# A third tile routine for an expert's last tokens: x stationary in column groups of TensorE, and the counts that choose it

## The chip, the core and the metric

The kernel runs on one core of a Trainium2 chip. The metric is the device time of one execution in microseconds (us); before the change the median of 4 runs is 718.03 us (716.1 to 719.92). All operands of the matrix products discussed here are float32.

## What is computed

Sliding-window causal attention (8 batches, 8 heads, 576 positions, head width 64, window 64) gives x with 4608 tokens of 512 numbers. Each token then goes to one of 8 experts, and its row passes through that expert's two weight matrices:

```python
logits = x @ w_gate                      # 4608 x 8
expert_idx = argmax(logits, axis=1)
gate_w = softmax(logits)[chosen]
for e in range(8):                       # x_e: the tokens of expert e
    h = maximum(x_e @ w1[e], 0.0)        # 512 -> 1024
    y_e = h @ w2[e]                      # 1024 -> 512
out = gate_w[:, None] * y                # in the tokens' own order
```

The inputs are drawn from a fixed seed. Counted from the reference with them, experts 0 to 7 get 669, 400, 748, 505, 592, 390, 566 and 738 tokens. In tiles of 256, expert by expert, the last tile holds 157, 144, 236, 249, 80, 134, 54 and 226 of them.

## The kernel before, in words

The first part, up to some 226 us, does the attention with PE (TensorE), ACT, DVE and POOL side by side, and writes x, weighted by the gate, to device memory (`x_dram`). It also counts the tokens of each expert (`count`), and `starts` (L216 to L225) turns the counts into numbers of tiles on DVE with small 128x8 instructions: per expert the number of whole tiles (`fulls_i`), of all tiles (`all_i`), the largest of these, and the place where each expert's tiles begin. Two tiles of expert 0 are worked in straight code, mixed with the end of the routing, among it the table of which token lies in which slot (`slot_table`: L839 to L864, read by PE at L854).

From some 272 us on, the rest of the tiles is chosen at run time. `expert(e)` (L1063) issues the loads of expert e+1's weights on SP's queue, does its first tile (none for expert 0, which has two already), and `more` (L1074) tests registers that hold the counts: is there another tile, and is it a whole one or a half one? Each test is a branch on every engine. Four places matter:

- **A whole tile** of 256 slots (`hidden`, `output`): seven products of half-size blocks for each of the two matrix products, with the sums of weight blocks formed beforehand by POOL (`sums_w1`, `sums_w2`: four instructions each) and the sums of x by DVE (`sums_x`, L333). The weights stand in TensorE (128 columns each) and x moves for the first product; the hidden values stand and the weights move for the second (L388).
- **A half tile** for up to 160 left-over tokens (`half_tile`, L436 to L477): plain products. For the first, w1 stands and 160 tokens move (L444). For the second, the 32 tokens behind the first 128 stand in one of four 32-column groups at a time while 128 columns of w2 move through each (L465); then the 128 tokens stand and all 512 columns of w2 move (L470). Both accumulate over the 8 blocks of the hidden width.
- **The feed for the next tile.** Inside tile n, DVE turns the rows of tile n+1 in 16 32x32-block transposes (`turned_blocks`, L315), ACT copies them into place (`keep_turned`, L327), DVE forms their sums (`sums_x`), and POOL then gathers the rows of tile n+2 into the buffer just turned (`gather`, L275). One buffer of rows exists, so the gather waits for the last transpose.
- **The results of the last tile.** At a tile's start `finish` (L425) adds the last product of the tile before on DVE (three L384 instructions); POOL scatters the rows to the output (`scatter`, L295) after it. Then, if it is the expert's second tile, POOL forms the sums of the next expert's w1, or, if it is an expert's first, those of its own w2.

The order on each engine is the order of the code; there is no scheduler. A float32 matmul has two records on PE in this trace and two on PEld (the loads of weights).

Of the kernel before, what the change touches and what calls it, by code (L numbers as in the profile page):

```python
# [13 lines left out]
I32 = mybir.dt.int32  # L14
AF = mybir.ActivationFunctionType
ALU = mybir.AluOpType
AX = mybir.AxisListType
# [19 lines left out]
def kernel(  # L37
# [34 lines left out]
    NW = 2  # L72
    QD = 32
    HALF = P + QD
    NCUT = NT // P
    assert D == WINDOW and 2 * D == P and NG * P == DM and NB * WINDOW == S
    assert S - SM == WINDOW and KB == NV + 1 and NTB * P == BG * S and B % BG == 0 and NTILE * TB <= 128 * P
# [10 lines left out]
    wg = consts.tile([P, NG, GE], F32, name="wg")  # L88
    nc.gpsimd.memset(wg[:], 0.0)
    perm_i = consts.tile([P, NS], I32, name="perm_i")  # L90
    info_i = consts.tile([P, 2 * E + 1], I32, name="info_i")
    fulls_i, all_i, most_i = info_i[:, 0:E], info_i[:, E : 2 * E], info_i[:, 2 * E :]

    places_i = consts.tile([P, E + 1], I32, name="places_i")
    perm_e = consts.tile([P, NE * C], I32, name="perm_e")
# [119 lines left out]

    def starts():  # L216

        for got, slots in ((fulls_i, TB - 1 - HALF), (all_i, TB - 1)):
            V.tensor_scalar(out=got, in0=count[:], scalar1=float(slots), scalar2=float(TB), op0=ALU.add, op1=ALU.max)
            V.tensor_single_scalar(got, got, TB.bit_length() - 1, op=ALU.arith_shift_right)  # L220
        V.tensor_copy(out=nt[:], in_=all_i)
        V.tensor_reduce(out=most_i, in_=nt[:], axis=AX.X, op=ALU.max)
        V.tensor_tensor_scan(out=cum[:], data0=ones[:, 0:E], data1=nt[:], initial=0.0, op0=ALU.mult, op1=ALU.add)
        V.tensor_tensor(out=start[:], in0=cum[:], in1=nt[:], op=ALU.subtract)
        V.tensor_single_scalar(chunk0[:], start[:], float(C), op=ALU.mult)  # L225

    zrow = consts.tile([1, DM], F32, name="zrow")
    nc.vector.memset(zrow[:], 0.0)
# [39 lines left out]
    def form_all(parts):  # L268
        for _ in parts:
            pass  # L270
# [165 lines left out]
    def half_tile(e, blocks, after, next_x):  # L436

        w1, w2 = w1s[e % NW], w2s[e % NW]
        f = 0
        for n, acc in enumerate(pps):  # L440
            f0 = f
            for i in range(acc.shape[1]):
                for g in range(NG):
                    nc.tensor.matmul(  # L444
                        acc[:, i], lhsT=w1[:, g, f * P : (f + 1) * P],
                        rhs=xq[:, g].rearrange("p c s -> p (c s)")[:, 0:HALF],
                        start=(i + g == 0), stop=(g == NG - 1), skip_group_check=True,
                    )
                f += 1
            if n == 1:  # L450
                some(blocks, 8)
                V.tensor_scalar_max(hp[:, f0:f], acc, 0.0)
            else:
                relu(out=hp[:, f0:f], in_=acc)
        V.memset(v1, 0.0)
        V.memset(yw2, 0.0)
        form_all(blocks)
        if after is not None:
            gather(perm_i[:, after])

        quad = lambda c: slice(c * QD, (c + 1) * QD)
        y = y2(0, P)
        for f in range(FT):
            for c in range(NQ):
                nc.tensor.matmul(  # L465
                    y[quad(c)], lhsT=hp[:, f, P:], rhs=w2[:, f, c * P : (c + 1) * P], start=(f == 0), stop=(f == FT - 1),
                    skip_group_check=True,
                )
        for f in range(FT):
            nc.tensor.matmul(yps[0], lhsT=hp[:, f, 0:P], rhs=w2[:, f, :], start=(f == 0), stop=(f == FT - 1))  # L470
        for c in range(NQ):
            copy = V.tensor_copy if c % 2 else nc.scalar.copy
            to = ys[1] if c < NQ // 2 else v3
            copy(out=to[0:QD, c % 2 * P : (c % 2 + 1) * P], in_=y[quad(c)])
        if next_x:
            keep_turned()
            sums_x([xn[:, c] for c in range(C)])  # L477

    def body(e, last, after, full, between=None, next_x=True):

        finish()
        scatter(perm_i[:, last])
        if between is not None:
            between()
        blocks = turned_blocks() if next_x else iter(())
        if not full:
            half_tile(e, blocks, after, next_x)
            return
        form_all(hidden(e, blocks))
        parts = output(e, blocks, next_x)  # L490
        next(parts)
        if after is not None:
            gather(perm_i[:, after])
        form_all(parts)

    with tc.manual_schedule(), ExitStack() as held, ExitStack() as brief:
# [371 lines left out]

        def loads():

            _, n = nc.values_load_multi_w_load_instructions(info_i[0:1, :], min_val=0, max_val=NT // P)
            _, places = nc.values_load_multi_w_load_instructions(
                places_i[0:1, :], engines=(mybir.EngineType.Pool,), min_val=0, max_val=NTILE,
                skip_runtime_bounds_check_because="sums of numbers of tiles, at most NTILE for any tokens",
            )
            return [(n[e], n[E + e], places[e]) for e in range(E)], places[E], n[2 * E]

        def after(s, routing, bg):

# [174 lines left out]
    with tc.manual_schedule():  # L1054
        load_w1(1)
        load_w2(1)
        def at(n):
            n = nc.s_assert_within(
                n, 0, NTILE - 1, skip_runtime_bounds_check_because="a tile with a token is one of the NTILE"
            )  # L1060
            return lambda ahead: bass.ds((n + ahead) * C, C)

        def expert(e):  # L1063

            fulls, tiles, first = regs[e]
            if 0 < e < E - 1:
                load_w1(e + 1)
                load_w2(e + 1)

            def one(n, full, between=None):  # L1070
                slots = at(first + n)
                body(e, slots(0), slots(3), full, between)

            def more(n, between=None):  # L1074

                with tc.If(tiles > n) as some_left:  # L1076
                    with tc.If(fulls > n, preferred_fallthrough_block=False) as full:
                        one(n, True, between)
                        if n + 1 < KT:
                            more(n + 1)  # L1080
                    with full.Else():
                        one(n, False, between)
                if between is not None:
                    with some_left.Else():
                        between()

            if e:
                one(0, True, partial(sums_w2, e))
            more(1 if e else NE, partial(sums_w1, e + 1) if e + 1 < E else None)

        def any_number():

            tiles_of = v_m(2080, E, NTILE)
            V.tensor_tensor(
                out=tiles_of, in0=_inner(cum[:], NTILE), in1=_ins(lane[:, 0:NTILE], 1, E), op=ALU.is_le
            )
            with nc.allow_low_precision("integers"):
                V.tensor_reduce(out=expert_i[:], in_=tiles_of.rearrange("p e t -> p t e"), axis=AX.X, op=ALU.add)
            _, (tiles,) = nc.values_load_multi_w_load_instructions(
                places_i[0:1, E : E + 1], min_val=0, max_val=NTILE,  # L1100
                skip_runtime_bounds_check_because="a sum of numbers of tiles, at most NTILE for any tokens",
            )
            with tc.For_i(NE, tiles) as i:
                _, (e,) = nc.values_load_multi_w_load_instructions(
                    expert_i[0:1, bass.ds(i, 1)], engines=(mybir.EngineType.SP,), min_val=0, max_val=E - 1,
                    skip_runtime_bounds_check_because="a tile that is numbered belongs to an expert",
                )
                for w, view in ((w1s[0], w1v), (w2s[0], w2v)):
                    nc.sync.dma_start(out=w[:], in_=view[bass.ds(e, 1)].rearrange("o p n d -> (o p) n d"))
                sums_w1(0)  # L1110
                sums_w2(0)
                slots = at(i)
                gather(perm_i[:, slots(1)])
                form_all(turned_blocks())
                keep_turned()
                sums_x([xn[:, c] for c in range(C)])
                form_all(hidden(0))
                form_all(output(0, iter(()), False))
                finish()
                scatter(perm_i[:, slots(1)])  # L1120

        with tc.If(most < KT + 1) as few:  # L1122
            for e in range(E):
                expert(e)
            finish()
            scatter(perm_i[:, bass.ds(end * C, C)])
        with few.Else():
            finish()
            scatter(perm_i[:, NE * C : (NE + 1) * C])
            any_number()  # L1130
# [28 lines left out]
```

## Time and profile before

| what | value |
|---|---|
| median of 4 runs | 718.03 us |
| the profiled execution, own time | 715.61 us |
| its span, first to last instruction | 713.9 us |
| granted TensorE clock, mean | 0.995 |
| PE busy | 687.6 us (96%) |
| DVE / ACT / POOL busy | 503.5 / 259.7 / 355.8 us |
| half tiles | 5: 64 records of L444 each, 320 in all |

How to read it: the profile lists busy time by engine, then groups of instructions by line with count, busy time and mean duration. A line of a timeline gives the start, the time from the first start to the last end of a run of equal instructions, the engine, the line, the operation, output and inputs, shape, count, and in brackets the idle time before it with what ended that. Matmuls overlap in PE's pipeline, so what one costs is the distance between starts, not its duration.

### The profile page before, as it was taken

How to read it: one execution, taken by the hardware profiler on the slowest of the kernel's cores; microseconds unless marked ns; L12 is line 12 of the kernel's file. 1: busy time of each engine (PE TensorE's matmuls, PEld its weight loads, DVE VectorE, ACT ScalarE, POOL GpSimd, SP SyncE). 2: the span in 40 equal slices, each digit the busy share in tenths (PEclk: the TensorE clock that was granted, in tenths of full speed). 3: DMA queues.
4: the chain of work that ended last, by engine and by line, in shares of the span. 5: the costliest groups of instructions: out<-in, count | busy, mean ns of one | idle time of the engine just before them, and what ended most of it. 6: DMA issues, size and time to landing. Idle time of an engine off the chain costs nothing. (4 is left out here: it accounts for less than half of the span.)

```text
span 713.9 us, 17980 instructions
## 1 busy us (share of the span) xinstructions
PE 687.6 (96%) x6882; PEld 606.5 (85%) x6882; DVE 503.5 (71%) x1656; ACT 259.7 (36%) x655; POOL 355.8 (50%) x366
## 2 busy tenths in 40 slices
PE   5999999999879999999999999999999999999995
PEld 3788888888769898897999999899989799979995
DVE  3576898898966858676776686677667586666864
ACT  4688888888745111211111121111111121112210
POOL 4223748559674016847462356446274756263012
PEclk9999999999999999999999999999999999999999
DMA  8998889979542373716201531450271621111011
GB/s 158 220 203 184 173 174 235 211 165 238 164 157 92 100 268 118 228 60 237 79 31 61 167 130 58 145 184 30 68 268 60 202 101 43 61 38 51 11 61 58
DMA packets 137608, 94.42 MB, mean 132 GB/s; under 512 B 117072, under 2 KB 117072, under 8 KB 137490
## 3 DMA queue, kind: packets, MB, share of 16 engines
q1 hardware_dynamic: 127858, 62.16, 33.0%
q0 software_dynamic: 9056, 28.58, 12.5%
q10 hardware_dynamic: 576, 2.10, 0.9%
q8 instruction: 74, 1.21, 0.7%
q14 instruction: 44, 0.36, 0.2%
HBM read 73.94 MB, written 20.45 MB: 132 GB/s over the span
## 5 line engine op out<-in xcount | busy, mean ns | idle before, releaser
L315 DVE STREAM_TRANSPOSE v_m<-qk_m 32x256 f32<-32x256 f32 x320 | 139.3, 435 | 8.4 <-DMA qk_m<-x_dram,at_g 2.5
L275 POOL DMA_INDIRECT qk_m<-x_dram,at_g x42 | 45.5, 1083 | 176.1 <-DVE v_m L315 147.1
L344 PE MATMUL bank<-qk_m,s 128*128 128x128 f32 x1024 | 122.5, 275 | 0.5 <-DVE qk_m L365 0.5
L344 PEld LDWEIGHTS bank<-qk_m,s 128*128 128x128 f32 x1024 | 118.3, 192 | 0.7 <-issue 0.7
L651 ACT ACTIVATE pr<-pr,mx 128x128 f32<-128x128 f32 x288 | 89.6, 390 | 31.6 <-DVE mx L641 31.6
L344 PE MATMUL bank<-qk_m,w 128*128 128x128 f32 x768 | 93.8, 275 | 0.9 <-PEq L1076 0.7
L344 PEld LDWEIGHTS bank<-qk_m,w 128*128 128x128 f32 x768 | 90.6, 192 | 4.4 <-issue 4.1
L641 DVE CUSTOM_DVE_ANT_0 pr<-bank,mask 128x128 f32<-128x128 f32 x288 | 64.4, 286 | 27.4 <-PE bank L628 26.0
L384 DVE TENSOR_TENSOR v_m<-bank,v_m 128x256 f32<-128x256 f32 (+1 forms) x95 | 43.8, 480 | 40.8 <-PE bank L388 25.9
L295 POOL DMA_INDIRECT out_dram<-v_m,at_s x42 | 42.6, 1014 | 54.1 <-DVE v_m L384 49.9
L569 POOL COPY v_m<-v_m 64x520 f32<-64x520 f32 x32 | 19.9, 621 | 70.6 <-DMA v_m<-in_v_dram 67.9
L140 POOL TENSOR_TENSOR s<-w 128x1024 f32<-128x1024 f32 x22 | 52.2, 2373 | 0.0
L674 PEld LDWEIGHTS bank<-v_m,pT 128*64 128x64 f32 x1152 | 41.1, 140 | 10.9 <-DVE xs L688 4.9
L674 PE MATMUL bank<-v_m,pT 128*64 128x65 f32 x1152 | 47.8, 231 | 2.2 <-DVE xs L688 2.2
L351 ACT COPY qk_m<-bank 128x512 f32<-128x512 f32 x16 | 9.4, 587 | 108.6 <-PE bank L344 63.1
L388 PE MATMUL bank<-qkT_m,v_m 128*128 128x256 f32 x216 | 48.3, 379 | 0.0
L388 PEld LDWEIGHTS bank<-qkT_m,v_m 128*128 128x128 f32 x216 | 41.0, 190 | 5.5
L327 ACT COPY qk_m<-v_m 128x512 f32<-128x512 f32 x40 | 22.7, 615 | 62.4 <-DVE v_m L315 62.4
L628 PE MATMUL bank<-qkT_m 64*64 64x128 f32 x1152 | 44.9, 287 | 0.1
L444 PEld LDWEIGHTS bank<-qk_m,w 128*128 128x128 f32 x320 | 43.9, 190 | 0.9 <-issue 0.7
L444 PE MATMUL bank<-qk_m,w 128*128 128x160 f32 x320 | 44.4, 299 | 0.4 <-ACT qk_m L327 0.4
L595 PE MATMUL bank<-ident,qk_m 128*128 128x128 f32 x256 | 36.8, 287 | 8.1 <-POOL mask L517 5.0
(174 smaller groups left out, 1250.8 us busy)
## 6 DMA issues: line engine op xcount, KB each, us to landing
w<-in_moe_w_dram SPq DMA_DIRECT2D x11, 2048.0 KB, 9.9
qk_m<-in_q_dram SPq DMA_DIRECT2D x72, 128.0 KB, 4.0
qk_m<-in_k_dram SPq DMA_DIRECT2D x72, 128.0 KB, 3.6
v_m<-in_v_dram SPq DMA_DIRECT2D x64, 128.0 KB, 4.3
qk_m<-in_moe_w_dram SPq DMA_DIRECT2D x3, 2048.0 KB, 10.4
x_dram<-xs POOLq DMA_DIRECT2D x6, 512.0 KB, 5.2
x_dram<-xs POOLq DMA_DIRECT2D x3, 768.0 KB
w<-in_moe_w_dram ACTq DMA_DIRECT2D x4, 512.0 KB, 4.1
```

Of the source, the lines that this page charges most:

```text
L140: op()
L275: G.indirect_dma_start(out=xg[c], out_offset=None, in_=x_dram[:, :], in_offset=bass.IndirectOffsetOnAxis(ap=at_g[:, c : c + 1], axis=0),)
L295: put = G.indirect_dma_start(out=out[:, :], out_offset=bass.IndirectOffsetOnAxis(ap=at_s[:, c : c + 1], axis=0), in_=ys[c], in_offset=None ...
L315: V.transpose(out=xn[b * QD : (b + 1) * QD, :, :, a * QD : (a + 1) * QD].rearrange("p c g i -> p (c g) i"), in_=rows[a * QD : (a + 1) * QD ...
L344: nc.tensor.matmul(acc[:, f, :], lhsT=a[:, g, f * P : (f + 1) * P], rhs=b[:, g, :], start=(first and f == 0 and g == 0), stop=(g == HG - 1 ...
L384: plus = lambda out, a, b: V.tensor_tensor(out=out, in0=a, in1=b, op=ALU.add)
L388: nc.tensor.matmul(acc, lhsT=a[:, f, :], rhs=b[:, f, :], start=(start and f == 0), stop=(stop and f == HF - 1), skip_group_check=True,)
L444: nc.tensor.matmul(acc[:, i], lhsT=w1[:, g, f * P : (f + 1) * P], rhs=xq[:, g].rearrange("p c s -> p (c s)")[:, 0:HALF], start=(i + g == 0 ...
L628: nc.tensor.matmul(out_, lhsT=qT[rows, t, a * WINDOW : (a + 1) * WINDOW], rhs=rhs, start=True, stop=True, skip_group_check=True,)
L641: V.tensor_tensor_reduce(out=prs[h][:, m, :], in0=scs[h][:, m, :], in1=mask[:, m0 + m, :], scale=-scale, scalar=-2 * MASKED, op0=ALU.add, ...
L651: nc.scalar.activation(out=y, in_=y, func=AF.Exp, scale=-1.0, bias=mx[:, h, m : m + 1])
L674: nc.tensor.matmul(px[a * D : (a + 1) * D, h, m, :], lhsT=pTs[h][:, m, a * D : (a + 1) * D], rhs=vt[:, h, :], start=True, stop=True, skip_ ...
```

## The change

`starts` now counts in thirds: `kinds_i` is the number of all tiles, plus the number of tiles that hold over 96 tokens, plus the number that hold over 160. So 3n+1 stands for a last tile with at most 96, 3n+2 for one with up to 160, 3n+3 for a whole one. `info_i` has 9 values instead of 17. `more` branches on the one number, with a third test between half and rest. And `rest_tile` does the last tile where at most 96 tokens are left: the first 64 of them in two column groups of 64 columns, the other 32 in four groups of 32.

```diff
+    REST = P - QD
-    info_i = consts.tile([P, 2 * E + 1], I32, name="info_i")
+    info_i = consts.tile([P, E + 1], I32, name="info_i")
+    parts_i = consts.tile([P, 2, E], I32, name="parts_i")
     def starts():
-        for got, slots in ((fulls_i, TB - 1 - HALF), (all_i, TB - 1)):
-            V.tensor_scalar(out=got, in0=count[:], scalar1=float(slots), scalar2=float(TB), op0=ALU.add, op1=ALU.max)
+        def tiles_over(got, rest):
+            V.tensor_scalar(
+                out=got, in0=count[:], scalar1=float(TB - 1 - rest), scalar2=float(TB), op0=ALU.add, op1=ALU.max
+            )
             V.tensor_single_scalar(got, got, TB.bit_length() - 1, op=ALU.arith_shift_right)
-        V.tensor_copy(out=nt[:], in_=all_i)
-        V.tensor_reduce(out=most_i, in_=nt[:], axis=AX.X, op=ALU.max)
+        tiles_over(kinds_i, 0)
+        V.tensor_copy(out=nt[:], in_=kinds_i)
         V.tensor_tensor_scan(out=cum[:], data0=ones[:, 0:E], data1=nt[:], initial=0.0, op0=ALU.mult, op1=ALU.add)
         V.tensor_tensor(out=start[:], in0=cum[:], in1=nt[:], op=ALU.subtract)
         V.tensor_single_scalar(chunk0[:], start[:], float(C), op=ALU.mult)
+        for n, rest in enumerate((REST, HALF)):
+            tiles_over(parts_i[:, n], rest)
+            V.tensor_tensor(out=kinds_i, in0=kinds_i, in1=parts_i[:, n], op=ALU.add)
+        V.tensor_copy(out=e_m[:], in_=kinds_i)
+        V.tensor_reduce(out=most_i, in_=e_m[:], axis=AX.X, op=ALU.max)
...
+    def rest_tile(e, blocks, after, next_x):
+        w1, w2 = w1s[e % NW], w2s[e % NW]
+        def rows(acc, tokens, ways):
+            n, width = P // ways, FF // ways
+            for g in range(NG):
+                for c in range(ways):
+                    nc.tensor.matmul(
+                        acc[c * n : (c + 1) * n, 0:width], lhsT=xq[:, g, 0, tokens],
+                        rhs=w1[:, g, c * width : (c + 1) * width], start=(g == 0), stop=(g == NG - 1),
+                        skip_group_check=True,
+                    )
+        a, b = banks[0](0, FF // 2), banks[1](0, FF // 4)
+        rows(b, slice(L, L + QD), 4)
+        relu(out=hr4, in_=b)
+        rows(a, slice(0, L), 2)
+        relu(out=hr, in_=a)
+        for h, t, acc in ((hr4, ht4, banks[3](0, HF // 2, P)), (hr, ht, banks[6](0, HF, P))):
+            for i in range(h.shape[1] // P):
+                nc.tensor.transpose(out=acc[:, i], in_=h[:, i * P : (i + 1) * P], identity=ident[:])
+            nc.scalar.copy(out=t.rearrange("p i c s -> p i (c s)"), in_=acc)
+        V.memset(v1, 0.0)
+        V.memset(yw2, 0.0)
+        form_all(blocks)
+        if after is not None:
+            gather(perm_i[:, after])
+        y, y4 = banks[7](0, DM), y2(0, P)
+        for f in range(FT):
+            for c in range(4):
+                nc.tensor.matmul(
+                    y4[c * QD : (c + 1) * QD], lhsT=ht4[:, f % (HF // 2), f // (HF // 2)],
+                    rhs=w2[:, f, c * P : (c + 1) * P], start=(f == 0), stop=(f == FT - 1), skip_group_check=True,
+                )
+        for f in range(FT):
+            for c in range(2):
+                nc.tensor.matmul(
+                    y[c * L : (c + 1) * L, c * HM : (c + 1) * HM], lhsT=ht[:, f % HF, f // HF],
+                    rhs=w2[:, f, c * HM : (c + 1) * HM], start=(f == 0), stop=(f == FT - 1), skip_group_check=True,
+                )
+        for c in range(4):
+            nc.scalar.copy(out=yps[0][L : L + QD, c * P : (c + 1) * P], in_=y4[c * QD : (c + 1) * QD])
+        if next_x:
+            keep_turned()
+            sums_x([xn[:, c] for c in range(C)])
+        nc.scalar.copy(out=yps[0][0:L, hi_], in_=y[L:, hi_])
+        V.tensor_copy(out=yps[0][0:L, lo_], in_=y[0:L, lo_])
...
-                with tc.If(tiles > n) as some_left:
-                    with tc.If(fulls > n, preferred_fallthrough_block=False) as full:
-                        one(n, True, between)
+                with tc.If(kind > 3 * n) as some_left:
+                    with tc.If(kind > 3 * n + 2, preferred_fallthrough_block=False) as full:
+                        one(n, whole_tile, between)
                         if n + 1 < KT:
                             more(n + 1)
                     with full.Else():
-                        one(n, False, between)
+                        with tc.If(kind > 3 * n + 1) as half:
+                            one(n, half_tile, between)
+                        with half.Else():
+                            one(n, rest_tile, between)
```

Here P is 128, QD 32, L 64, FF 1024, DM 512, NG 4, FT 8, HM 256. In the rest tile the first product runs with x standing, so the hidden values come out with tokens in rows; six TensorE transposes (two for the 32 tokens, four for the 64) turn them back for the second product.

More of the change, by code (lines that the diff above doesn't have):

```diff
@@ L90 @@
     perm_i = consts.tile([P, NS], I32, name="perm_i")
-    info_i = consts.tile([P, 2 * E + 1], I32, name="info_i")
-    fulls_i, all_i, most_i = info_i[:, 0:E], info_i[:, E : 2 * E], info_i[:, 2 * E :]
+    info_i = consts.tile([P, E + 1], I32, name="info_i")
+    kinds_i, most_i = info_i[:, 0:E], info_i[:, E:]
+    parts_i = consts.tile([P, 2, E], I32, name="parts_i")
     places_i = consts.tile([P, E + 1], I32, name="places_i")
@@ L477, in half_tile @@
             sums_x([xn[:, c] for c in range(C)])
-    def body(e, last, after, full, between=None, next_x=True):
+    L = P // 2
+    hr, hr4 = qk_m(8192, FF // 2), qk_m(8192 + FF // 2, FF // 4)
+    ht, ht4 = qk_m(8960, HF, 2, L), qk_m(8960 + HF * P, HF // 2, 4, QD)
+    def rest_tile(e, blocks, after, next_x):
[43 more added lines that the diff above has]
+        V.tensor_copy(out=yps[0][0:L, lo_], in_=y[0:L, lo_])
@@ L481, in body, with whole_tile @@
+    def whole_tile():
+        pass
+    def body(e, last, after, tile_, between=None, next_x=True):
         finish()
@@ L485, in body @@
         blocks = turned_blocks() if next_x else iter(())
-        if not full:
-            half_tile(e, blocks, after, next_x)
+        if tile_ is not whole_tile:
+            tile_(e, blocks, after, next_x)
             return
@@ L869, in loads @@
         def loads():
-            _, n = nc.values_load_multi_w_load_instructions(info_i[0:1, :], min_val=0, max_val=NT // P)
+            _, n = nc.values_load_multi_w_load_instructions(info_i[0:1, :], min_val=0, max_val=3 * NT // P)
             _, places = nc.values_load_multi_w_load_instructions(
@@ L875, in loads @@
             )
-            return [(n[e], n[E + e], places[e]) for e in range(E)], places[E], n[2 * E]
+            return list(zip(n[0:E], places[0:E])), places[E], n[E]
         def after(s, routing, bg):
@@ L1063, in expert @@
         def expert(e):
-            fulls, tiles, first = regs[e]
+            kind, first = regs[e]
             if 0 < e < E - 1:
@@ L1068, in expert, with one @@
                 load_w2(e + 1)
-            def one(n, full, between=None):
+            def one(n, tile_, between=None):
                 slots = at(first + n)
-                body(e, slots(0), slots(3), full, between)
+                body(e, slots(0), slots(3), tile_, between)
             def more(n, between=None):
-                with tc.If(tiles > n) as some_left:
-                    with tc.If(fulls > n, preferred_fallthrough_block=False) as full:
-                        one(n, True, between)
+                with tc.If(kind > 3 * n) as some_left:
+                    with tc.If(kind > 3 * n + 2, preferred_fallthrough_block=False) as full:
+                        one(n, whole_tile, between)
                         if n + 1 < KT:
@@ L1087, in expert @@
             if e:
-                one(0, True, partial(sums_w2, e))
+                one(0, whole_tile, partial(sums_w2, e))
             more(1 if e else NE, partial(sums_w1, e + 1) if e + 1 < E else None)
@@ L1120, in any_number @@
                 scatter(perm_i[:, slots(1)])
-        with tc.If(most < KT + 1) as few:
+        with tc.If(most < 3 * KT + 1) as few:
             for e in range(E):
```

## The prediction

> **What bounds the kernel now.** I read the page's busy times first, then the busy time by stretches for four tiles of the experts' part, then the timelines of PE and of all engines around the tiles that would change.
>
> The page's line of busy times, and the stretches (the half tiles of experts 4 and 6, then a whole tile; columns: length, busy time and instructions of PE, PEld, DVE, ACT, POOL, granted clock, DMA share, GB/s):
>
> ```profile
> PE 687.6 (96%) x6882; PEld 606.5 (85%) x6882; DVE 503.5 (71%) x1656; ACT 259.7 (36%) x655; POOL 355.8 (50%) x366
> ```
>
> ```profile
> 506.05:523.70 17.65, 17.65 (x146) 13.45 (x145) 11.63 (x28) 2.56 (x6) 5.36 (x7) 1.00 0.49 177
> ...
> 615.12:632.76 17.64, 17.64 (x146) 13.44 (x144) 11.63 (x28) 2.56 (x6) 5.36 (x7) 1.00 0.19 62
> 657.35:681.95 24.60, 24.60 (x170) 23.15 (x169) 17.08 (x35) 4.59 (x8) 4.64 (x7) 1.00 0.15 44
> ```
>
> In these stretches PE has no idle time, and no other engine is full. A microsecond of PE taken from a tile is taken from the end, as long as what the next tile needs is ready earlier by as much.
>
> Which half tiles change? The counts say experts 4 (80 left over) and 6 (54). The timeline agrees on the order: the three whole tiles at 632.76, 657.35 and 681.95 are expert 7's 738 tokens, so the half tile at 615.12 is expert 6's; going back, 548.29 is expert 5's and 506.05 expert 4's. PE in the latter, from its timeline:
>
> ```profile
> 506.05 8.86 PE L444 MATMUL bank<-qk_m,w 128*128 128x160 f32 x64
> 514.84 1.95 PE L465 MATMUL bank<-qk_m 128*32 128x128 f32 x64
> 516.73 7.13 PE L470 MATMUL bank<-qk_m 128*128 128x512 f32 x16
> 523.70 1.95 PE L344 MATMUL bank<-qk_m,w 128*128 128x128 f32 x16
> ```
>
> By starts: 8.79 for the first product, 1.89 for 32 tokens of the second, 6.97 for 128 tokens; 17.65 together.
>
> **The rest tile on PE.** L465 is the key: 64 records of 128 columns in 1.89 us, 0.030 each, while L344's records of 128 columns that fill the array start 1.78/16 = 0.111 apart (523.70 to 525.48). Four column groups thus run 3.8 times as fast as one after the other. Two groups of 64 columns are not in the expert part, but attention has them, L674, with 65 columns moving:
>
> ```profile
> 123.66 0.97 PE L674 MATMUL bank<-v_m,pT 128*64 128x65 f32 x24
> 124.56 0.42 PE L711 MATMUL bank<-xT,wg 128*32 128x128 f32 x6
> ```
>
> 24 records in 0.90 us are 0.0375 each. L388's 256 columns take 1.73/8 = 0.216 (536.20 to 537.93), so 65 would take 0.055 alone: L674 has some overlap, a factor of 0.68, not the full 0.5. But it puts four records into one group before it turns to the other, and its records are short; the rest tile changes groups at every matmul, as L465 does. I take the full overlap by L465, the nearer in order and length, and keep 0.68 and 1.0 as worse ends. By parts:
>
> - 32 tokens, first product: 16 matmuls, 32 records of 256 columns in fours: 8 x 0.216 = 1.73.
> - 64 tokens, first product: 8 matmuls, 16 records of 512 columns in pairs, each 6.97/16 = 0.436 by L470: 8 x 0.436 = 3.49.
> - Six transposes: L659's six in attention take 0.71 (129.07 to 129.78): 0.71.
> - A new wait. The four transposes of the 64 tokens need relu over 128x512, and it needs the last matmul. That matmul ends 0.592 - 0.436 = 0.16 after PE could go on; ACT starts some 0.09 later (by L454 after L444), takes 0.60 (L358) and PE resumes about 0.07 later; two transposes and a change of groups, some 0.35, lie beside it. PE idles 0.6 (0.4 to 0.9). The other handovers are covered: relu of the 32 lies under the 64's matmuls, the copies of the transposed values under the transposes and the 32's second product.
> - 32 tokens, second product: the shape of L465, 1.89.
> - 64 tokens, second product: 16 matmuls, 32 records of 256 columns in pairs: 16 x 0.216 = 3.46.
> - Changes of groups: L444's 64 starts are 0.136 apart, 8.70, and L465 starts after 8.79, so a change costs about 0.1. Five beyond L465's own: 0.5.
>
> Sum 12.4, against 17.65: 5.3 a tile, 10.5 for two.
>
> [...]
>
> **What must keep up.** A tile of 12.4 us leaves the others 5.3 less.
>
> - DVE: `finish` ends 0.9 after the tile's start (506.25 + 0.69), two memsets take 0.6, 16 block transposes 7.3 (3.62 + 3.66): turned at 8.8. In the half tile half of them waited behind L452; now nothing stands between.
> - ACT: the four copies of the 32 tokens wait for their second product, which ends near 9, and take about 1.2 (L474, 0.26 each); `keep_turned` behind them 1.13, to 11.4. PE needs it at 12.4: covered by 1.0. `sums_x` on DVE ends near 12.7; the first two sums, which the next tile's second product needs at 14.2, are there at 11.8.
> - Two last copies come after PE's end, ACT 0.4, then DVE 0.4 (the build lets DVE wait for ACT), so `finish` of the next tile ends at about +2.4 in it instead of +0.9. DVE's next is L354, which waits for PE until +3.84 (527.54). Covered.
> - POOL: the scatters wait for `finish`, 3.7 after the next tile's start instead of 2.2, and the four sums of w2 behind them end at +13.2 instead of +11.6; PE needs the last at +14.2 (537.93). Covered by 1.0.
> - The gather starts at 8.9 instead of 12.5, 3.4 ahead of PE's end. The load of expert 6's w1 on SP starts once PE is done with w1, 5.4 after the start instead of 9.3, and lands 9 to 10 us later, beside the gather. With such a load in flight gathers took 6.5 to 7 us to land (518.52 to 525.51), so these land between 15.5 and 17.5; the next tile's blocks want them at 12.4 + 4.4 = 16.8. Being late by 1.5 cost PE 0.5 once in this trace (idle before the matmuls at 300.90, DVE having waited until 295.71). I take 0, with 0.5 as the end.
> - The branch: a rest tile is reached by a jump, as a whole tile is, which costs PE nothing visible here; the dearest branch in this part cost 0.7 (at 456.79, where a skipped tile's semaphore is waited for). Neither changed tile has that wait. I take 0; 1.4 for two is the end.
>
> **The counts.** `starts` has 14 instructions on DVE instead of 9:
>
> ```profile
> 229.10 0.17 DVE L225 TENSOR_SCALAR chunk<-start 128x8 f32<-128x8 f32 x1
> 229.18 0.69 DVE L370 TENSOR_TENSOR qk_m<-v_m,bank 128x512 f32<-128x512 f32 x1
> ...
> 232.16 0.68 DVE L840 TENSOR_REDUCE base<-of 128x36 f32<-128x288 f32 x1
> 233.43 0.69 DVE L140 TENSOR_TENSOR v_m<-qk_m 128x512 f32<-128x512 f32 x1 [0.60 <-ACT qk_m L376]
> ```
>
> Each that needs the one before starts 0.2 after it (227.93 to 228.42 and on); the five more, nearly all dependent, add 1.0 before L370. ACT's relu after L370 stands at 230.43, behind other work, and would move to 230.87; the copy at 234.25, for which PE waits, moves by the same 0.44, and so do L140 and the table that PE waits for at 238.70 and 240.25. DVE's idle 0.60 takes the rest. So 0.4 is lost here. The bounds are 0 and 1.0. Fewer registers to load change nothing: the loads at 237 to 268 us hold no PE up.
>
> **Sum.** 715.61 - 10.5 + 0.4 = 705.5 by the profiled execution. The runs shown have a median 2.4 above it, so I forecast 718.03 - 10.1 = **707.9**.
>
> **Rivals.**
>
> - *Two column groups overlap only as in L674.* The paired stages become 0.68 of one after the other: 4.74 + 4.70 instead of 3.49 + 3.46, 2.5 more a tile: 707.9 + 5.0 = 712.9. For: the only two-group row. Against: its order and its short records.
> - *They do not overlap: slower.* If the second group waits for the first, 16 x 0.436 + 32 x 0.216 = 13.9 instead of 6.95; the tile takes 19.3, 1.7 more than the half tile: 718.03 + 3.4 + 0.4 = 721.8. It turns slower once the paired stages lose over 5.1 of the 6.95 gained by pairing. For: L465 has only 32-column groups. Against: L674 is below one after the other already.
> - *A follower becomes the bound*: POOL's sums of w2, the gather, or `keep_turned`, each with about 1 us to spare. If one is 2.5 late, about 1.5 of it reaches PE, twice: 707.9 + 3 = 710.9.
> - *Only one tile, or none, takes the new path.* By the counts, 80 and 54 are well under 96. One tile would give 713.2.
>
> **Chances.** The forecast, 705 to 710 with its small ends, 0.72; L674's overlap 0.13; a late follower 0.07; no overlap 0.06; one tile 0.02. Times 704.5 to 713.5 hold all but the slower case and a stretch on both sides. About 0.5% (3.6 us) is what a measurement of this kernel can tell from no change: faster 0.89, within 0.05, slower 0.06.
>
> **What would show it.** In the profile after: the matmuls of 160 columns (L444) x192 instead of x320; two tiles of 12 to 13 us on PE, in them the 512-column records 0.22 apart on average and the 256-column ones of the second product 0.11 (right), or 0.30 and 0.15 (L674), or 0.44 and 0.22 (no overlap); one idle time of about 0.6 before the transposes; and no idle time of PE in the 15 us after each of the two tiles. `starts` should end about 1.0 later and L854 0.4. I am wrong if PE waits in the next tile for POOL's sums, for the blocks or for ACT's copies by more than 1 us.

## The result, and the profile after

| | before | after |
|---|---|---|
| median of the runs | 717.71 us (78 runs, 715.01 to 723.1) | 719.85 us (52 runs, 717.12 to 724.3) |
| the profiled execution: span | 713.9 us | 719.2 us |
| PE busy | 687.6 us | 680.6 us |

The ratio after to before is 1.0029, with a 95% interval of 1.002 to 1.0039. The change made the kernel 2.1 us slower, where 10.1 us less were forecast. That is 0.3%, within what the prediction called no change, though over so many runs the interval leaves out 1. PE works 7 us less, so the rest tile does save work, and what it saves is lost as idle time.

Busy times of the page after:

```profile
PE 680.6 (95%) x6894; PEld 593.8 (83%) x6894; DVE 504.4 (70%) x1657; ACT 263.0 (37%) x665; POOL 355.8 (49%) x366
```

Four stretches of it (length, busy time and instructions of PE, PEld, DVE, ACT, POOL, granted clock, DMA share, GB/s): expert 3's last whole tile, the time behind it, and the two rest tiles:

```profile
434.63:459.23 24.60, 24.60 (x169) 22.96 (x167) 16.32 (x33) 4.59 (x8) 13.65 (x10) 1.00 0.14 45
459.23:474.13 14.90, 6.10 (x33) 5.68 (x33) 1.45 (x3) 0.59 (x1) 11.48 (x7) 0.66 0.88 316
519.75:532.28 12.53, 12.13 (x151) 6.51 (x151) 9.62 (x23) 3.83 (x10) 4.47 (x6) 1.00 0.37 130
625.05:637.58 12.53, 11.96 (x150) 6.51 (x151) 9.61 (x23) 3.83 (x10) 4.14 (x6) 1.00 0.19 69
```

The rest tiles are what was forecast: 12.5 us instead of 17.65, a small wait ahead of each included. The second row is the surprise. Behind a tile that the change does not touch, PE works 6.1 of 14.9 us, at a granted clock of 0.66. That is more than the two rest tiles save. PE's timeline there (start, length, engine, line, operation, shapes, count, idle time before and what ended it):

```profile
457.50 1.89 PE L398 MATMUL bank<-w,v_m 128*128 128x256 f32 x8
462.81 0.98 PE L354 MATMUL bank<-qk_m,w 128*128 128x128 f32 x3 [3.42 <-issue]
469.17 3.14 PE L354 MATMUL bank<-qk_m,w 128*128 128x128 f32 x13 [5.38 <-issue]
472.10 2.19 PE L354 MATMUL bank<-qk_m,s 128*128 128x128 f32 x16
474.13 1.95 PE L354 MATMUL bank<-qk_m,w 128*128 128x128 f32 x16
```

and at the same place before the change:

```profile
454.18 1.89 PE L388 MATMUL bank<-w,v_m 128*128 128x256 f32 x8
456.79 2.02 PE L344 MATMUL bank<-qk_m,w 128*128 128x128 f32 x16 [0.72 <-PEq L1076]
458.65 1.95 PE L344 MATMUL bank<-qk_m,s 128*128 128x128 f32 x16
460.44 1.95 PE L344 MATMUL bank<-qk_m,w 128*128 128x128 f32 x16
```

From the start of expert 3's last product to that of expert 4's third group of sixteen are 474.13 - 457.50 = 16.63 us after, and 460.44 - 454.18 = 6.26 before: **10.4 us** are lost. "issue" means that PE waited for nothing that the profile shows: no semaphore, no buffer, no transfer of data. It stopped once before its first matmul, again behind the third of sixteen, and the 13 records after that came 2.93/13 = 0.225 us apart, where 0.111 is normal.

What PE's sequencer did there, from the view of the line of `more`'s first test (duration in ns as minimum/median/maximum, first and last start):

```profile
L1143 PEldq COMPARE_BRANCH  x14: 65/76/4272, 270.3 to 683.7; - x14
...
L1143 PEldq EVENT_SEMAPHORE  x1: 51/51/51, 459.7 to 459.7; - x1
```

The single semaphore is the case of expert 3: 505 tokens are two whole tiles, so the test for a third tile fails, and the "no more tiles" path waits until PE's own last matmul is done (459.7). Only then does PE branch to the next expert's code, with nothing left queued. In `before` the same wait is the 0.72 of L1076. The branch behind the wait is what differs. After the change (in ns):

```profile
L1143 PEldq COMPARE_BRANCH  x1: 2747/2747/2747, 459.9 to 459.9; - x1
```

and before:

```profile
L1076 PEldq COMPARE_BRANCH  x1: 190/190/190, 456.4 to 456.4; - x1
```

It takes 2.75 us instead of 0.19. The 4272 ns in the row of the fourteen are the test ahead of it, from 455.4 on, when PE still had expert 3's last products to do.

The compiled programs say what lies between (blocks of PE's code in order of address, for the second and third tile of an expert):

```
before: [.. whole 3rd] [no 3rd] [no 2nd] [join]
after:  [half 3rd] [whole 3rd] [rest 3rd] [no 3rd] [rest 2nd] [no 2nd] [join]
```

"Join" is where the next expert's code begins. Before, it lay just behind the path that waits. After, `rest_tile` for the second tile lies between, some 302 records of PE and PEld by the rest tiles' rows (151 and 151), and the branch has to go over it. It is a tile that no expert takes in this run: both rest tiles are third tiles.

### The profile page after: what moved, and what is told of

Its sections match the earlier page's. It is cut to its first block, busy times and chain, and to the rows that moved or that the text cites. A ratio compares the mean times of both kernels' runs of the same rounds, so it can differ in the third digit from the quotient of the medians.

```text
span 719.2 us, 18007 instructions
## 1 busy us (share of the span) xinstructions
PE 680.6 (95%) x6894; PEld 593.8 (83%) x6894; DVE 504.4 (70%) x1657; ACT 263.0 (37%) x665; POOL 355.8 (49%) x366
## 3 DMA queue, kind: packets, MB, share of 16 engines
q8 instruction: 83, 1.36, 0.8%
## 5 line engine op out<-in xcount | busy, mean ns | idle before, releaser
L354 PE MATMUL bank<-qk_m,w 128*128 128x128 f32 x768 | 96.2, 279 | 9.2 <-issue 9.2
L354 PEld LDWEIGHTS bank<-qk_m,w 128*128 128x128 f32 x768 | 92.0, 195 | 13.2 <-issue 12.8
L364 DVE TENSOR_TENSOR qk_m<-bank,qk_m 128x512 f32<-128x512 f32 x16 | 11.1, 692 | 51.3 <-PE bank L354 47.9
L726 PE MATMUL bank<-ident,pr 128*128 128x128 f32 x288 | 42.6, 285 | 0.0
## 6 DMA issues: line engine op xcount, KB each, us to landing
w<-in_moe_w_dram SPq DMA_DIRECT2D x11, 2048.0 KB, 10.5
```

Source lines behind the costliest of these rows:

```text
L354: nc.tensor.matmul(acc[:, f, :], lhsT=a[:, g, f * P : (f + 1) * P], rhs=b[:, g, :], start=(first and f == 0 and g == 0), stop=(g == HG - 1 ...
L726: nc.tensor.transpose(out=tr[:, m, :], in_=prs[h][:, m, :], identity=ident[:])
```

## The experiments

**Theory: the far join.** The stall comes from where the blocks lie. How is a supposition: after a branch made with PE's queue empty, to a place far ahead, PE would stand until its code is there. **Rival theories:** the rest tiles themselves bring it (what they leave behind, or the counts), or the two loads of expert 5's weights, which start there (316 GB/s in the row above), are to blame.

### The rest tile only where it is a third tile

```diff
-                        with tc.If(kind > 3 * n + 1) as half:
+                        if n < KT - 1:
                             one(n, half_tile, between)
-                        with half.Else():
-                            one(n, rest_tile, between)
+                        else:
+                            with tc.If(kind > 3 * n + 1) as half:
+                                one(n, half_tile, between)
+                            with half.Else():
+                                one(n, rest_tile, between)
```

> The kernel after, but the rest tile exists only as an expert's third tile (n = 2); a second tile with few tokens takes the half tile. Both tiles that took the rest path are third tiles, so the work done is the kernel after's. What changes is the layout: after, the 81 PE instructions of the rest block for the second tile stand between the block that ends expert 3's path (no third tile: wait for PE's own last matmul, then a branch) and the join at the start of the next expert; here they are gone, as in the kernel before. Far-join theory: the 11.1 us that PE lost after 459.2 us fall back to the 0.7 of before, and the time is 719.85 - 10.4 = about 709.5 (ratio to before 0.987 to 0.991). Rival, the program as a whole became too long for its fetches: eight of the fifteen rest blocks are still there, so at least half of the 11 stays, 714 or more. Rival, the rest tiles themselves lose the time elsewhere: no change, 719 to 720.

Measured: 707.42 us (704.64 to 708.7), 717.53 before; ratio 0.9836 (0.9796 to 0.9876). PE's timeline at expert 3's end:

```profile
455.33 1.89 PE L398 MATMUL bank<-w,v_m 128*128 128x256 f32 x8
457.97 2.02 PE L354 MATMUL bank<-qk_m,w 128*128 128x128 f32 x16 [0.75 <-PEq L1143]
```

The recorded ratio is a little below that of the two medians (0.986). With the unused blocks of the second tiles left out (one for each expert but expert 0) the stall is gone, the branch behind the wait takes 0.19 us again, the wait for PE's own end is back at 0.75, and the time is the one forecast for the change. No tile that this run executes has been taken out: experts 4 and 6 still take the rest tile.

### No tile takes the rest tile, its code stays

```diff
-        for n, rest in enumerate((REST, HALF)):
+        for n, rest in enumerate((0, HALF)):
```

> The kernel after with the threshold of the rest tile at 0 instead of 96, so that the code and its layout stay and no expert takes the rest path: five half tiles as before. Far-join theory: the stall at expert 3's end stays and the two tiles' 10.5 us are not gained, so 719.85 + 10.3 = about 730 (ratio to before 1.015 to 1.019). Rival, the rest tiles bring the loss with them (by what they leave late for the next tile): the time falls back to that of before plus 0.4 for the counts, 718.

Measured: 729.66 us (726.56 to 731.54); ratio 1.0158 (1.011 to 1.0206).

```profile
461.02 0.57 PE L354 MATMUL bank<-qk_m,w 128*128 128x128 f32 x3 [3.22 <-issue]
467.38 3.14 PE L354 MATMUL bank<-qk_m,w 128*128 128x128 f32 x13 [5.79 <-issue]
```

The stall is there without a single rest tile executed. With the run before this separates the two halves of the change: the rest tiles save some 10 us (729.66 to 719.85), and the place of their code costs some 12 (719.85 to 707.42).

### No loads at the stall

Leaves out the two loads of expert 5's weights, so expert 5 is computed with expert 3's.

```diff
-            if 0 < e < E - 1:
+            if 0 < e < E - 1 and e != 4:
```

> The kernel after without the two loads of expert 5's weights (4 MB), which SP issues at expert 3's end; expert 5 is computed with the weights that stand in that buffer, expert 3's, all instructions of the engines are the same. Theory that the instruction fetch after the far branch queues behind these loads: the branch still costs a fetch, some 1.5 to 3 us, but the second stall of 5.4 us after three matmuls goes; 719.85 - 6 to 9 = 711 to 714. Rival, the fetch is slow by itself and the loads do not matter: PE still stands for 3.4 and 5.4 us there, 719 to 720.

Measured: 716.68 us (714.88 to 718.97); ratio 0.9989 (0.9969 to 1.001). A miss: most of the stall stayed.

```profile
461.83 0.57 PE L354 MATMUL bank<-qk_m,w 128*128 128x128 f32 x3 [3.72 <-issue]
465.46 3.14 PE L354 MATMUL bank<-qk_m,w 128*128 128x128 f32 x13 [3.05 <-issue]
```

The stretch of the stall in this kernel (columns as above):

```profile
459.00:468.00 9.00, 3.11 (x15) 2.96 (x16) 0.83 (x2) 0.00 (x0) 7.98 (x5) 0.69 0.16 60
```

The DMA share is 0.16, where it was 0.88 in the stall of the changed kernel, and PE still waits 3.72 and 3.05 us. The loads lengthen the second wait only (5.38 to 3.05). From the last product to the third group are 14.33 us instead of 16.63, so the loads make up some 2 of the 10.4.

### Before, with its join moved away

The kernel before, with no rest tile in it; the "no more tiles" paths are laid ahead of the blocks of the tiles.

```diff
-                with tc.If(tiles > n) as some_left:
+                with tc.If(tiles > n, preferred_fallthrough_block=False) as some_left:
```

> The kernel before with one change: the test whether there is another tile has its false block laid first, so the false block is next to the test, and the join lies behind the half and whole blocks of the third tile (160 PE instructions) instead of directly behind. No rest tile, no other counts. Far-join theory: expert 3's end waits for PE's last matmul and then branches far, and PE loses about 11 us there as in the kernel after: 717.7 + 10 = about 728 (ratio 1.012 to 1.017). Rival, the loss belongs to the rest code or the larger program: 717 to 718, ratio 1.00.

Measured: 723.68 us (722.71 to 727.26); ratio 1.009 (1.0056 to 1.0124).

```profile
456.61 1.89 PE L388 MATMUL bank<-w,v_m 128*128 128x256 f32 x8
462.31 2.42 PE L344 MATMUL bank<-qk_m,w 128*128 128x128 f32 x16 [3.81 <-issue]
464.52 3.22 PE L344 MATMUL bank<-qk_m,s 128*128 128x128 f32 x16
467.58 2.08 PE L344 MATMUL bank<-qk_m,w 128*128 128x128 f32 x16
```

The join moved away, alone, in the old kernel: a stall at the same place. The size was expected at twice this. Here there is one wait of 3.81 us and not two, and from the last product to the third group are 467.58 - 456.61 = 10.97 us instead of 6.26, a loss of 4.7. Why the join's place costs one wait here and two in the changed kernel is taken up below, with the times of the packets of code.

### The tests nested the other way

All rest tiles are kept, and their blocks moved ahead of the others, so that the join is near again.

```diff
-                    with tc.If(kind > 3 * n + 2, preferred_fallthrough_block=False) as full:
-                        one(n, whole_tile, between)
-                        if n + 1 < KT:
-                            more(n + 1)
-                    with full.Else():
-                        with tc.If(kind > 3 * n + 1) as half:
+                    with tc.If(kind > 3 * n + 1, preferred_fallthrough_block=False) as over_rest:
+                        with tc.If(kind > 3 * n + 2, preferred_fallthrough_block=False) as full:
+                            one(n, whole_tile, between)
+                            if n + 1 < KT:
+                                more(n + 1)
+                        with full.Else():
                             one(n, half_tile, between)
-                        with half.Else():
-                            one(n, rest_tile, between)
+                    with over_rest.Else():
+                        one(n, rest_tile, between)
```

> The kernel after with all its rest tiles, also for second tiles, but the tests nested the other way round: rest block first, then half, then whole with the next tile in it. So every rest block lies ahead of the blocks that end an expert's path, and these are again directly ahead of the join. Far-join theory: expert 3's end costs 0.7 as before, so 719.85 - 10.4 = about 709 or a little less, ratio to before 0.983 to 0.990, as with the rest block of the second tile taken out. Rival, the number of far branches matters wherever they lie: a whole tile now takes two forward branches over other blocks, and if these are not hidden under queued matmuls each costs 2.7 to 4.3 us, so 715 or more. Rival, a rest block for the second tile is itself the cost: 719 to 720.

Measured: 736.33 us (733.94 to 740.31), 717.91 before; ratio 1.026 (1.0223 to 1.0297). By the time the first rival was right. At expert 3's end the far-join theory got only half of what it said:

```profile
463.56 0.57 PE L354 MATMUL bank<-qk_m,w 128*128 128x128 f32 x3 [0.61 <-PEq L1143]
466.35 3.14 PE L354 MATMUL bank<-qk_m,w 128*128 128x128 f32 x13 [2.21 <-issue]
```

The branch behind the wait takes 0.19 us again and the first wait is gone. The second, behind three matmuls, is still there. With the slow records behind it 5.2 us are lost: 472.53 - 461.06 = 11.47 from the last product to the third group, instead of 6.26. So the distance to the join decides the first wait, but not, or not alone, the second.

The waits of PE for issue in this kernel (what was waited for: us in total, times, longest):

```profile
PE bank L354 <- issue: 13.6, 8, 4.7
```

and the branches of the inner test, L1145:

```profile
L1145 PEldq COMPARE_BRANCH  x15: 64/3554/6100, 269.8 to 725.5; - x15
```

Before the change, the test of the same meaning (is it a whole tile?) had

```profile
L1077 PEldq COMPARE_BRANCH  x19: 67/343/6406, 267.7 to 702.7; - x19
```

so single branches of up to 6.4 us stood there too, and yet PE's waits for issue in that whole trace come to 0.2 us: a long branch cost next to nothing here as long as the matmuls queued ahead of it lasted. The branch of 6.41 us starts at 559.0, and L470's sixteen records of 512 columns keep PE busy until 566.1. One of 4.03 at 377.9, with records of 256 columns ahead of it, left the wait of 0.18 that makes up those 0.2. In the nested form a whole tile goes over the rest block and then over the half block, and the median of the second test is 3.55 us. PE then waits for issue in eight places, and 5.4 us in two more that the view puts down to DVE's results. The longest is at the last whole tile:

```profile
695.25 1.89 PE L398 MATMUL bank<-w,v_m 128*128 128x256 f32 x8
701.86 3.78 PE L354 MATMUL bank<-qk_m,w 128*128 128x128 f32 x16 [4.72 <-issue]
```

There both tests were long (4.54 and 3.96 us). At the other six whole tiles behind two tests the first took 0.3 to 0.6 and the second 3.5 to 5.2, so it was not simply the number of branches that cost time; what each has to pass over was not varied by itself.

### The counts moved out of the way

To the kernel with rest tiles as third tiles only, and to the one above, one edit was added: the eight DVE instructions that form `kinds_i`'s parts go to a function of their own, `kinds()`, called behind the slot table; `starts` keeps the six that the table needs.

```diff
+    def kinds():
         for n, rest in enumerate((REST, HALF)):
...
+        kinds()
```

> The rest tile as a third tile alone (as in the run before), and the eight DVE instructions that make the kinds out of the counts moved from the counting of the tiles to behind the slot table, so that the instructions ahead of the chain to that table are 6 instead of 14 (9 in the kernel before). If those instructions cost what was worked out (0.4 us by way of ACT's relu and copy), PE's wait for ACT's copy of the first product of the second stage goes from 0.56 to 0.1 or 0.2, and the table's matmuls start 0.4 to 0.6 earlier after tile 0's start; the time falls by the same, to 0.982 to 0.988 of before. Rival, DVE has slack there and ACT's wait comes from other work: the wait stays at 0.5.

Measured: 707.7 us (704.66 to 713.36); ratio 0.9869 (0.9831 to 0.9907). By the times this can't be told from the kernel without the edit (0.9836, 0.9796 to 0.9876). The trace shows the small gain: in the changed kernel PE waits for ACT's copy,

```profile
237.49 1.99 PE L398 MATMUL bank<-qk_m 128*128 128x256 f32 x8 [0.55 <-ACT v_m L412]
```

and with the edit that wait is gone:

```profile
236.74 1.99 PE L401 MATMUL bank<-qk_m 128*128 128x256 f32 x8
```

> Both changes together: rest tiles for every place, laid ahead of the path ends, and the kinds made behind the slot table. Far-join theory and the counts' cost: 717.6 - 10.4 to 11.0, about 707, ratio 0.982 to 0.988, with no stretch without PE work over 1 us after 226 us. Rival (forward branches not hidden): 714 or more.

Measured: 735.98 us (734.31 to 738.93); ratio 1.0261 (1.0234 to 1.0289). A miss in the same direction as the nested tests alone, for the same reason: PE waits for issue 18.4 us in ten places.

The kernels that beat both are the two in which the rest tile is a third tile only, at 1.3 to 1.6% below before by the ratios, 1.4% by the medians. For other counts of tokens their price is that a second tile with at most 96 left stays a half tile.

## Why the prediction was wrong

**The step that failed is "The branch".** It said that a rest tile "is reached by a jump, as a whole tile is, which costs PE nothing visible here", named the 0.7 at 456.79 as the dearest branch in this part, and dismissed it since "neither changed tile has that wait. I take 0; 1.4 for two is the end". For the rest tiles' own branches that nearly held: 0.25 and 0.28 us stand ahead of the two, 0.45 behind the second, within its end of 1.4. The mistake was to ask only what the new tiles pass through. New code also moves what lies behind it, and the one branch that PE makes with an empty queue, the one at 456.79, goes over just that code. There PE lost 10.4 us more than before. No rival had it, so the range ended 6 us below the median.

The sum, against the profile before, by starts of PE's groups:

| term | forecast | measured |
|---|---|---|
| two rest tiles, 12.29 each for 17.65 | -10.5 | -10.7 |
| counts: first tile's product to tile 1 | +0.4 | +0.5 |
| branch at expert 3's end | 0 | +10.4 |
| small waits around and behind the rest tiles | 0 | +2.6 |
| the end, behind the last tile's products | 0 | -0.3 |
| sum | -10.1 | +2.5 |
| difference of the medians | | +2.1 |

The two profiled spans differ by 5.3; another 2.3 of that lies ahead of the change (the first tile's product starts at 227.02 instead of 224.72; other kernels with the same code there had 225.5 to 226.8), and 0.5 is spread over the other tiles.

**The rest tile on PE** was right in nearly every part. The first rest tile, expert 4's, in PE's timeline:

```profile
519.99 5.52 PE L501 MATMUL bank<-w,qk_m 128*32 128x256 f32 x48
525.44 0.44 PE L514 MATMUL bank<-ident,qk_m 128*128 128x128 f32 x2
526.20 0.66 PE L514 MATMUL bank<-ident,qk_m 128*128 128x128 f32 x4 [0.33 <-ACT qk_m L511]
526.79 1.95 PE L525 MATMUL bank<-qk_m 128*32 128x128 f32 x64
528.68 3.67 PE L531 MATMUL bank<-qk_m 128*64 128x256 f32 x32
532.28 2.05 PE L354 MATMUL bank<-qk_m,w 128*128 128x128 f32 x16
```

(The row of 48 records merges both first products, 32 records of 256 columns and 16 of 512.) The second product of the 64 tokens, L531, takes 3.60 for 32 records, 0.1125 each, where 0.108 is full overlap of two groups and 0.216 none. Both first products together take 5.45, against 1.73 + 3.49 and two changes of groups at 0.1. So attention's 0.68 does not carry over, and both rivals on the overlap are out. That its order or its short records made it 0.68 stays likely and untested. The one new wait, before the four transposes, is 0.33 instead of 0.6.

If all of the 0.23 left over in the first products (5.45 less 1.73 + 3.49) is two changes of groups, each took 0.12, where 0.1 was taken. In L531 two groups ran 0.216/0.1125 = 1.92 times as fast as one after the other, 0.96 of the full overlap.

**The followers.** `keep_turned` and POOL's sums were in time, as said. The gather behind expert 4's rest tile was late, as its end of the range allowed; DVE's row and then PE's:

```profile
538.57 2.68 DVE L325 STREAM_TRANSPOSE v_m<-qk_m 32x256 f32<-32x256 f32 x6 [1.66 <-DMA qk_m<-x_dram,at_g]
```

```profile
543.76 2.02 PE L354 MATMUL bank<-qk_m,s 128*128 128x128 f32 x16 [0.49 <-DVE qk_m L375]
```

Taking 0 with 0.5 as the end was too low: the next whole tile lasted 557.71 - 532.28 = 25.43 instead of 24.59, 0.84 more. The whole tile behind expert 6's rest tile lasted 662.97 - 637.58 = 25.39, 0.80 more, with a wait of 0.45 for issue in it. The other 1.0 of the 2.6 comes in pieces of 0.1 to 0.4 at the borders of the tiles around. So the sign "no idle time of PE in the 15 us after each of the two tiles" failed at both.

**The counts**: 0.51 by the distance from the first tile's last product of x to tile 1 (227.02 to 249.37 after; 224.72 to 246.56 before), 0.44 forecast, and none with `kinds` moved.

**What is shown and what is argued.** That the place of the code makes the stall is shown. Blocks that no tile takes bring it, leaving out the ones in the way takes it away, and moving the join alone brings a smaller one in the old kernel. The nested kernel shows that the distance to the join is not all of it.

That PE waited for its code is argued from times in the traces. The pages list a DMA queue q8 of the kind "instruction": 83 packets and 1.36 MB after, 16 KB each, and the trace has the time of each packet. At expert 3's end (us; "branch" is the one behind PE's wait for its own end):

| kernel | branch | packet on q8 landed | PE went on | later by |
|---|---|---|---|---|
| before | 0.19 | during PE's work | 456.79 | |
| rest tile as third tile only | 0.19 | during PE's work | 457.97 | |
| after, first wait | 2.75 | 461.28 | 462.81 | 1.53 |
| after, second wait | | 467.78 | 469.17 | 1.39 |
| no tile takes it, first wait | 2.79 | 459.51 | 461.02 | 1.51 |
| no tile takes it, second wait | | 465.93 | 467.38 | 1.45 |
| no loads, first wait | 3.23 | 460.14 | 461.83 | 1.69 |
| no loads, second wait | | 464.13 | 465.46 | 1.33 |
| before, join moved away | 3.46 | 460.78 | 462.31 | 1.53 |
| nested, second wait | 0.19 | 464.96 | 466.35 | 1.39 |

Each of these waits ends 1.3 to 1.7 us behind a packet. So do all seven branches of over 1 us that PE's sequencer made before the change (1.35 to 1.51), and all ten after it (1.32 to 1.62), whether PE then stood still or not. The times also fit a double stall. In the changed kernel PE did three matmuls and stood still again, and the next packet landed 6.50 us behind the first; without the loads, 3.99. In the old kernel with its join moved away the next packet landed at 467.27, while PE was still at work. The number of packets says little: q8 has 74 before, 83 after and 78 with the rest tile as third tile only, but also 74 with the join moved away, which stalls.

No run changed the way the code comes in, so this link rests on the times; at expert 3's end the waits for issue were 2.21 to 5.79 us a piece. Why PE stopped behind the third matmul at the join was not measured.

## What to carry to other kernels

Code that is chosen at run time cost time here even where it was never chosen (10.8 us, 472.93 - 455.91 less 6.26, at expert 3's end with no rest tile executed): ask of every branch, not only of the new ones, how far it goes in the compiled order and what is still queued when it is taken. Before the change a long branch was nearly free as long as queued matmuls lasted (branches of up to 6.4 us, 0.2 us of waiting for issue in all). At expert 3's end, where PE had just drained, a stall cost 4.7 to 10.8 us. In the nested kernels, where whole tiles go over two blocks, PE waited 14 to 18 us for issue in all. So keep a rare block out of the way of the path that waits, and let the common case go over as little code as it can. Moving the rare block elsewhere is not enough by itself: in the nested kernels that brought waits to the whole tiles.

## What was not expected of the hardware

- A long branch was followed by two waits. PE did three matmuls at the join, then waited 5.38 us more, to 1.39 us behind the next packet on q8; without the two loads beside it, 3.05.
- A second loss stood beside the idle time: with the 3.42 and 5.38 us of waiting the granted clock of the stretch was 0.66 (0.50 from 462.36 to 472.60) and thirteen records ran at half pace, 1.5 us more. In the nested kernel, behind waits of 0.61 and 2.21, 29 records took 2.9 us more (6.18 from 466.35 to 472.53). That the waiting lowers the clock was not shown: no run varied it alone.
- The branches of one test took from 0.067 to 6.4 us before the change, and nearly all of that was hidden. A branch record's length by itself did not give its cost: 6.41 us at 559.0 left PE no wait, with matmuls queued to 566.1, and after the change 2.75 us at 459.9, with nothing queued, a wait of 3.42.
